# Keeping half a granule more between two layers: folded w2, packed tiny tiles, rows in a lent annex, and V as the weight around a turn

## The chip, the cores and the metric

The kernel runs on one core of one Trainium2 chip; the chip's other cores do nothing for it. The metric is the device time of one execution in microseconds (us), less is better. TensorE is the matmul engine, VectorE and ScalarE the two elementwise engines, GpSimd the small general one; the DMA engines, sixteen for the core, bring data from HBM, the chip's main memory, into SBUF, the core's own memory. PSUM is the small memory that TensorE writes its results to.

## The reference, cut to what matters

The model is two layers over the same caches: attention of one query token over 4096 cached keys and values, 32 heads, 8 batch rows, then a small feed-forward block. The second round reads the same caches and weights as the first.

```python
B, Sq, D = 8, 1, 640
Hq, Hkv, Sk, Dh = 32, 32, 4096, 128
...
x = x + _A_ref(_layernorm(x), k_cache, v_cache, wq, wo)   # layer 0
x = x + _B_ref(_layernorm(x), w1, w2)                     # Dff = 1728
x = x + _A_ref(_layernorm(x), k_cache, v_cache, wq, wo)   # layer 1, same caches
x = x + _B_ref(_layernorm(x), w1, w2)
```

The caches hold 537 MB in bf16, so reading them once per layer is 1074 MB. What is still in SBUF when layer 1 of a batch row begins need not be read again.

## The kernel before

The caches pass through an arena of 26 slots in SBUF. A slot holds a granule: a quarter of the keys (or of the values) of a pair of heads, 4 KB on each of 128 partitions, 512 KB in all. A visit is one pair of heads of one batch row in one layer: it takes four granules of K, makes a softmax, then takes four of V. A Python function plans everything ahead: the order of visits, which slot each load goes into, and how many granules one load takes.

The **turn** of a batch row is where its layer 1 begins. The pairs visited last in layer 0 are visited first in layer 1, in reversed order. At a turn 21 granules stay in the arena and 3 more are stashed in PSUM banks and a 2 KB annex, so for a while only five slots are free and loads are single granules. In this document t is the first visit of a turn, and t+4 the fifth. The kernel has eight turns; seven of them lie between two batch rows, and per-turn means are over these seven.

```python
order1 = list(range(NP - 1, NP - 4, -1)) + list(range(NP - 3))
...
moving = [not any(t - AHEAD - 1 <= i < t + 5 for t in turns) and i < NV - 2 for i in range(NV)]
direct = [i == NV - 1 or visits[i][0] == 0 and last_of[visits[i][:2]] == i for i in range(NV)]
...
keep = set(first[: G - SPARE])                       # 21 granules
stash = first[G - SPARE : G - SPARE + STASH]         # 3 more
```

A visit's K product is *wide* where `moving` is true (the cache streams as the moving operand, 4 matmuls of 512 columns a granule) and *narrow* near a turn (the cache is the weight, 16 matmuls of one column a granule). V is wide too, unless the visit is *direct*: then V is the weight. Each matmul comes with a weight load, so a wide granule costs 8 TensorE instructions and a narrow or direct one 32.

```python
if which == "V":
    for c in range(4):
        h, j = c // 2, g * VJ + c % 2 * CJ
        for n in range(CJ) if direct[i] else ():
            nc.tensor.matmul(o2_ps[h], lhsT=arena[...128x128 of V...], rhs=P_tiles[i][:, h, j + n : j + n + 1], ...)
        if direct[i]:
            continue
        nc.tensor.matmul(o_ps[32 * c : 32 * c + CJ, :], lhsT=P_tiles[i][:, h, j : j + CJ],
                         rhs=arena[...512 columns of V...], ...)
```

A wide V is evicted by ScalarE into a row tile (`o_sb`) and gathered by four matmuls; a wide K leaves its exponentials in a row tile too (`P_row`). Both rows share one buffer of 1 KB.

Of the kernel before, what the change touches and what calls it, by code (L numbers as in the profile page):

```python
# [16 lines left out]
UNIT = 4  # L17
GP = 4
# [17 lines left out]
def plan(B, NP, n_up, n_down):  # L36
# [5 lines left out]

    order0 = list(range(NP))
    order1 = list(range(NP - 1, NP - 4, -1)) + list(range(NP - 3))
# [12 lines left out]
    moving = [not any(t - AHEAD - 1 <= i < t + 5 for t in turns) and i < NV - 2 for i in range(NV)]  # L57
    last_of = {(layer, b): v for v, (layer, b, hp) in enumerate(visits)}
    direct = [i == NV - 1 or visits[i][0] == 0 and last_of[visits[i][:2]] == i for i in range(NV)]
# [7 lines left out]
    stash = first[G - SPARE : G - SPARE + STASH]  # L67
# [8 lines left out]
    for which, i in slots:  # L76
        layer, b, hp = visits[i]
        uses += [(which, i, g) for g in range(UNIT)]
        stream += [(which, i, g) for g in range(UNIT) if layer == 0 or (which, hp, g) not in keep | set(stash)]
# [26 lines left out]

    def place(x):

        return visits[x[1]][1], tile_at(NP, x[0], visits[x[1]][2]) * UNIT + x[2]
# [6 lines left out]
    def feed():  # L116

        while at[0] < len(stream):
            lead = clock[1] - clock[0]
            calm = (PACE * (nth[stream[at[0]]] - at[1]) - LATE - lead) / 1.2  # L120
            least = next((n for us, n in LEADS if lead >= us), 1)
            least = min(least, max(1, (G - len(kept) - 2) // 3))
            most = min(max(least, int(calm)), LEADS[0][1], max(1, (len(stream) - at[0]) // 2))
            least = min(least, most)
            b, p = place(stream[at[0]])
            n = 1
            while n < most and place(stream[at[0] + n]) == (b, p + n):
                n += 1
            least = min(n, least)
            u = next((u for n in range(n, least - 1, -1) if (u := room(n)) is not None), None)  # L130
            if u is None:
                return
            n = next(k for k in range(n, 0, -1) if room(k) == u)
            for k, (which, i, g) in enumerate(stream[at[0] : at[0] + n]):
                ops.extend(("weights",) + w for w in weights.pop(i, []) if which == "K")
                owner[u + k] = True
                where[which, i, g] = u + k
                if keeps(which, i, g):
                    kept[which, b, visits[i][2], g] = u + k
            at[0] += n  # L140
            clock[1] = max(clock[1], clock[0] + 1.4) + 0.1 + 1.2 * n
            lands[u : u + n] = [clock[1] + 2] * n
            ops.append(("load", b, p, n, u))
# [5 lines left out]
    def release(which, i, g):  # L149
        key = which, visits[i][1], visits[i][2], g  # L150
        u = where.pop((which, i, g), None)
        at[1] += 1
        if key in kept:
            if visits[i][0] == 0:
                return
            u = kept.pop(key)
        if visits[i][0] == 0 and stashed(which, i, g) is not None:
            ops.append(("stash", stashed(which, i, g), u))
        owner[u], freed[u] = False, at[1]
        x = uses[at[1] + SOON] if at[1] + SOON < len(uses) else None  # L160
        if x and visits[x[1]][0] and stashed(*x) is not None:
            u = where[x] = room(1)
            owner[u] = True
            lands[u] = clock[0] + 2
            ops.append(("unstash", stashed(*x), u))
        feed()
# [130 lines left out]
def kernel(  # L297
# [31 lines left out]
    f_sizes = [min(P, Dff - f * P) for f in range(FC)]  # L329
# [11 lines left out]
    annex = sm.tile([P, 2 * BANK], BF16, name="annex", bufs=1)  # L341
    lent = [2 * BANK]

    def temp(shape, dtype, name):

        if shape[1] == 1:
            return sm.tile(shape, dtype, name=name, bufs=1)
        n = int(np.prod(shape[1:])) * (2 if dtype == FP32 else 1)
        lent[0] -= -(-n // 16) * 16
        assert lent[0] >= 0  # L350
        t = annex[: shape[0], lent[0] : lent[0] + n]
        t = t.bitcast(FP32) if dtype == FP32 else t
        return t.rearrange("p (a b) -> p a b", a=shape[1]) if len(shape) == 3 else t
# [6 lines left out]
    w2_sb = wres.tile([P, FC, D], BF16, name="w2_sb")  # L360
# [5 lines left out]
    def load_weights(which, g=0):  # L366
        if which == "wq":
            nc.sync.dma_start(out=wq_sb[:, g], in_=wq_src[:, g])
        elif which == "wo":
            h0, h1 = g * 2 * GP, (g + 1) * 2 * GP  # L370
            nc.sync.dma_start(out=wo_sb[:, h0:h1, :], in_=wo_src[:, h0:h1, :])
        elif which == "w1":
            nc.sync.dma_start(out=w1_sb, in_=B_w1.rearrange("p (c f) -> p c f", c=DC))
        else:
            nc.sync.dma_start(out=w2_sb, in_=B_w2.rearrange("p (f n) -> p f n", f=FC))
# [41 lines left out]
    o2_ps = o_ps[:, :1], s_ps[:, 8 * NJ - 1 : 8 * NJ]  # L417
    per = GW // (2 * BANK)
    stash_ps = ps.tile([P, (STASH * per - 1) * 2 * BANK], BF16, name="stash_ps")
    stash = [stash_ps[:, n * 2 * BANK : (n + 1) * 2 * BANK] for n in range(STASH * per - 1)] + [annex]  # L420
    assert len(stash) > DC
# [35 lines left out]
    def inverse_root(out, s2, k):  # L457

        v = sm.tile([P, 4], FP32, name="root", bufs=1)
# [15 lines left out]
    def do_ws(closing):  # L475

        for n, hp in enumerate(closing):
            ws = sm.tile([P, 2], FP32, name="wsum", bufs=1)
# [52 lines left out]
    def finish_steps(layer, b):  # L531
# [13 lines left out]
        def up(k):  # L545
            for f in up_parts[k]:
                fs = f_sizes[f]
                for c in range(DC):
                    nc.tensor.matmul(
                        h[k][:fs, f, :], lhsT=w1_sb[:, c, f * P : f * P + fs], rhs=st["xf"][:, :, c],  # L550
                        start=(c == 0), stop=(c == DC - 1),
                    )
# [7 lines left out]
        def root():  # L560
            if layer:
                st["rstd"] = root_of_all(var_ps[:, :nb])
            else:
                st["rstd"] = sm.tile([P, 1], FP32, name="rstd", bufs=1)
                inverse_root(st["rstd"], var_ps[:, :1], 1.0)

        def relu(k=None):
# [3 lines left out]
            for rows, lo, hi in ((P, part[0], min(part[-1] + 1, n_full)), (Dff % P, n_full, part[-1] + 1)):  # L571
                if rows and lo < hi:
                    nc.vector.tensor_scalar(
                        out=st["hT"][:rows, lo:hi], in0=h[k or 0][:rows, lo:hi], scalar1=0.0, scalar2=None, op0=ALU.max
                    )

        def down(k):
            for c, f in [(k, f) for f in range(FC)] if layer == 0 else [(c, f) for f in up_parts[k] for c in range(DC)]:
                fs = f_sizes[f]
                nc.tensor.matmul(  # L580
                    y[:, c, :], lhsT=w2_sb[:fs, f, c * P : (c + 1) * P], rhs=st["hT"][:fs, f, :],
                    start=(f == 0), stop=(f == FC - 1),
                )

        def add():
            yT = y.rearrange("p c b -> p b c")
            if layer == 0:
                nc.vector.scalar_tensor_tensor(out=x, in0=yT, scalar=st["rstd"], in1=x, op0=ALU.mult, op1=ALU.add)
                s1 = sm.tile([P, 1], FP32, name="s1", bufs=1)
# [10 lines left out]
        def center():  # L600
            xc = sm.tile([P, 1, DC], FP32, name="xc", bufs=1)
# [3 lines left out]
            xlns[b] = sm.tile([P, 1, DC], BF16, name="xq", bufs=2)  # L605
# [3 lines left out]
        def root2():  # L609
            r = q_scale[b] = sm.tile([P, 2], FP32, name="q_scale", bufs=2)  # L610
# [12 lines left out]
    def do_stash(slot, u):  # L623
        for n, t in enumerate(stash[slot * per : (slot + 1) * per]):
# [6 lines left out]
    def do_unstash(slot, u):  # L631
        for n, t in enumerate(stash[slot * per : (slot + 1) * per]):
# [3 lines left out]
    def do_load(b, p, n, u):  # L636
        nc.sync.dma_start(out=arena[:, u * GW : (u + n) * GW], in_=A_kv[b, :, p * GW : (p + n) * GW])

# [10 lines left out]

    def do_q(b, hp):  # L650
        q_ps = st["q", b, hp] = q2_ps if hp == NP - 1 else q1_ps[:, 2 * (hp % 2) : 2 * (hp % 2) + 2]
# [21 lines left out]
    def do_mm(which, i, g, u):  # L673
        layer, b, hp = visits[i]
        at = u * GW
        if which == "V":
            for c in range(4):
                h, j = c // 2, g * VJ + c % 2 * CJ
                for n in range(CJ) if direct[i] else ():
                    nc.tensor.matmul(  # L680
                        o2_ps[h], lhsT=arena[:, at + (c * CJ + n) * Dh : at + (c * CJ + n + 1) * Dh],
                        rhs=P_tiles[i][:, h, j + n : j + n + 1],
                        start=(j + n == 0), stop=(j + n == NJ - 1),
# [26 lines left out]
    def do_m1(i):  # L710
        m_tiles[i] = sm.tile([P, 2], BF16, name="mrow")
# [12 lines left out]
    def do_m2(i):  # L724
        if moving[i]:
            nmax[i] = sm.tile([2, 2], BF16, name="diag")
# [4 lines left out]
        hmx = sm.tile([2, 1], FP32, name="hmx")  # L731
        nc.vector.tensor_reduce(out=hmx, in_=turn_ps, axis=AX.X, op=ALU.max)  # L732
        nmax[i] = sm.tile([2, 2], BF16, name="diag")
# [13 lines left out]
    def do_e(i):  # L747
        nm = sm.tile([P, 2], FP32, name="nmax")
        layer, b, hp = visits[i]
        less, more = (q_scale[b][:, 1:2], q_scale[b][:, 0:1]) if layer else (-inv_sqrt_dh, inv_sqrt_dh)  # L750
        if moving[i]:
            less, more = (less[:OR], more[:OR]) if layer else (less, more)
            nc.scalar.activation(out=nm[:OR, :1], in_=max_ps[:OR, :1], func=ACT.Copy, scale=less)  # L753
            P_rows[i] = sm.tile([P, BANK], BF16, name="P_row", tag="row", bufs=1)
# [30 lines left out]
    def do_i(i):  # L785
        L = sm.tile([P, 2], FP32, name="lsum")
# [3 lines left out]
        invL[i] = sm.tile([P, 2], FP32, name="invL", bufs=3)  # L790
        nc.vector.reciprocal(out=invL[i], in_=L)

    def do_oc(i):
        o_tiles[i] = sm.tile([P, CJ, Dh], BF16, name="o_sb", tag="row", bufs=1)
# [9 lines left out]
    def do_o(i):  # L804
# [3 lines left out]
        else:  # L808
            dst = oT[i] = sm.tile([P, 2], BF16, name="oT")
# [5 lines left out]
        for h, o in enumerate(o2_ps):  # L815
            nc.vector.tensor_tensor(out=dst[:, h : h + 1], in0=o, in1=L[:, h : h + 1], op=ALU.mult)

# [31 lines left out]
    does = dict(WS=do_ws, S=do_s, SM=do_sm, SC=do_sc, YC=do_yc, load=do_load, stash=do_stash, unstash=do_unstash, weights=load_weights, mm=do_mm, M1=do_m1, T=do_t, M2=do_m2, B=do_b, E=do_e,  # L849
                L=do_l, I=do_i, OC=do_oc, OG=do_og, O=do_o, W=do_w, Y=do_y, C=do_finish, Q0=do_q0, Q=do_q, QC=take_q, QZ=do_qz, PT=do_pt, PC=do_pc, clear=do_clear)  # L850

    with tc.manual_schedule(engines={ENG.PE, ENG.DVE, ENG.Activation, ENG.Pool, ENG.SP}):
# [4 lines left out]
        lent[0] = 2 * BANK  # L857
# [9 lines left out]
def _laid_out(A_x, A_k_cache, A_v_cache, A_wq, A_wo, B_w1, B_w2):  # L867
# [5 lines left out]
    NP, NJ, DC, NG, FC = H // 2, Sk // p, D // p, H // 2 // GP, -(-Dff // p)  # L873
    c = np.ascontiguousarray
    w2 = np.zeros((FC * p, D), B_w2.dtype)
    w2[:Dff] = B_w2
# [3 lines left out]
    for hp in range(NP):  # L880
# [9 lines left out]
        "B_w2": c(w2.reshape(FC, p, D).transpose(1, 0, 2)).reshape(p, -1),  # L890
# [26 lines left out]
```

## Time and profile before

Median 2341.5 us over 6 runs (2338.0 to 2343.1).

| what | value | view |
|---|---|---|
| span of the profiled run | 2343.0 us | page |
| bytes read from HBM | 988.08 MB | page, DMA queues |
| TensorE busy | 60% | page |
| steady stretch | 432 GB/s | windows |
| just before a turn | 395 GB/s in the turn shown | windows |

The page of the kernel before. The first lines give span and busy time; the next three cut the span into 40 slices (granted TensorE clock and DMA busy share in tenths, and GB/s); then the DMA queues (packets, MB, share of 16 engines) and the chain of work that ended last.

```profile
span 2343.0 us, 43024 instructions
PE 1398.6 (60%) x18748; PEld 591.4 (25%) x18748; DVE 496.7 (21%) x2022; ACT 426.3 (18%) x986; POOL 59.5 (3%) x296
...
PEclk9999999999999998555555555555555555555555
DMA  9999999999999999999999999999999999999997
GB/s 411 430 433 401 433 432 432 431 396 432 432 432 430 404 434 431 430 427 403 433 432 431 426 412 434 430 432 420 427 431 427 432 416 430 431 431 431 396 433 329
...
q1 hardware_dynamic: 76564, 988.12, 99.4%
q8 instruction: 146, 2.39, 0.4%
q14 instruction: 43, 0.35, 0.0%
...
DMA 71%; PE 17%; ACT 6%; DVE 3%; issue 2%; SPq 0%; POOL 0%; ACTq 0%; DVEq 0%; POOLq 0%
```

The DMA engines are busy in every slice, and the slices between turns, the first and last aside, stay at 426 to 435 GB/s on both sides of the halved clock; the regular dips are the turns. The profiled run itself took 2344.8 us, longer than any of the six timed runs.

The groups of instructions of the kernel before: line, engine, operation, tiles and shapes, count, then busy us and mean ns of one, then idle before them. L687 is wide V, L680 direct V (one of its two halves), L795 the eviction of V.

```profile
L687 PE MATMUL o_ps<-arena,P_sb 128*4 128x512 bf16 x3952 | 584.3, 596 | 402.0 <-DMA arena<-in_A_kv_dram 401.0
L795 ACT CAST o_sb<-o_ps 100x512 bf16<-100x512 f32 x247 | 144.9, 587 | 289.3 <-PE o_ps L687 286.0 <-PE small_ps L781 2.5
L680 PE MATMUL o_ps<-P_sb,arena 128*128 128x1 bf16 x288 | 12.9, 166 | 7.5 <-DMA arena<-in_A_kv_dram 4.3 <-ACT o_sb L795 3.0
```

### The profile page before, as it was taken

The numbers are of one execution on the slowest core, as the hardware profiler recorded it, in microseconds if no ns is written. First come the engines' busy times: TensorE is split into PE (matmuls) and PEld (weight loads), VectorE is DVE, ScalarE is ACT, GpSimd is POOL, SyncE is SP. The second block draws the span as 40 slices with busy tenths as digits, with TensorE's granted clock in tenths as the row PEclk, the third lists the DMA queues.
The fourth block names the chain that finished last, engine by engine and source line by source line (L and its number), as shares of the span: only waits on it lengthen the run. The fifth ranks groups of instructions, "written<-read, shape, count | busy, mean of one in ns | idle before, by whom it ended". The sixth has DMA issues, their size and how long they took to land.

```text
span 2343.0 us, 43024 instructions
## 1 busy us (share of the span) xinstructions
PE 1398.6 (60%) x18748; PEld 591.4 (25%) x18748; DVE 496.7 (21%) x2022; ACT 426.3 (18%) x986; POOL 59.5 (3%) x296
## 2 busy tenths in 40 slices
PE   3547654576545764557545675556755567545766
PEld 1214211152111511125111241113411133111523
DVE  1113211131112211122111221112211122111312
ACT  1111211122111221112211121111211112111211
POOL 0000000000000000000000000000000000000000
PEclk9999999999999998555555555555555555555555
DMA  9999999999999999999999999999999999999997
GB/s 411 430 433 401 433 432 432 431 396 432 432 432 430 404 434 431 430 427 403 433 432 431 426 412 434 430 432 420 427 431 427 432 416 430 431 431 431 396 433 329
DMA packets 76753, 990.87 MB, mean 423 GB/s; under 512 B 8596, under 2 KB 8596, under 8 KB 36500
## 3 DMA queue, kind: packets, MB, share of 16 engines
q1 hardware_dynamic: 76564, 988.12, 99.4%
q8 instruction: 146, 2.39, 0.4%
q14 instruction: 43, 0.35, 0.0%
HBM read 988.08 MB, written 0.01 MB: 422 GB/s over the span
## 4 chain that ended last, share of the span: by engine, by line
DMA 71%; PE 17%; ACT 6%; DVE 3%; issue 2%; SPq 0%; POOL 0%; ACTq 0%; DVEq 0%; POOLq 0%
DMA arena<-in_A_kv_dram 71%; PE o_ps L687 5%; PE s_ps L695 4%; PE s_ps L705 2%; ACT P_row L755 2%; ACT o_sb L795 1%; PE small_ps L655 1%; DVE mrow L713 1%; ACT P_sb L761 1%; PE small_ps L800 1%; ACT arena L634 1%; PE small_ps L768 1%; PE small_ps L825 1%; DVE hmx L732 0%; ACT nmax L753 0%
## 5 line engine op out<-in xcount | busy, mean ns | idle before, releaser
L687 PE MATMUL o_ps<-arena,P_sb 128*4 128x512 bf16 x3952 | 584.3, 596 | 402.0 <-DMA arena<-in_A_kv_dram 401.0
L695 PE MATMUL s_ps<-arena,qz 128*4 128x512 bf16 x3040 | 410.3, 602 | 261.1 <-DMA arena<-in_A_kv_dram 249.5
L687 PEld LDWEIGHTS <-P_sb 128*4 128x4 bf16 x3952 | 107.4, 88 | 502.8 <-issue 491.7
L713 DVE TENSOR_REDUCE mrow<-s_ps 100x1 bf16<-100x512 f32 x190 | 131.8, 694 | 323.2 <-PE s_ps L695 323.2
L795 ACT CAST o_sb<-o_ps 100x512 bf16<-100x512 f32 x247 | 144.9, 587 | 289.3 <-PE o_ps L687 286.0
L753 ACT ACTIVATE nmax<-small_ps 100x1 f32<-100x1 f32 x106 | 18.1, 171 | 774.5 <-PE small_ps L742 774.5
L775 DVE CAST P_sb<-small_ps 128x64 bf16<-128x64 f32 x190 | 42.6, 224 | 523.1 <-PE small_ps L768 523.1
L695 PEld LDWEIGHTS <-qz 128*4 128x4 bf16 x3040 | 63.9, 85 | 313.7 <-issue 295.5
L705 PEld LDWEIGHTS <-arena 128*128 128x128 bf16 x4224 | 129.6, 104 | 40.8 <-DMA arena<-in_A_kv_dram 23.4
L705 PE MATMUL s_ps<-qo,arena 128*128 128x1 bf16 x3712 | 123.7, 165 | 17.2 <-ACT P_sb L761 7.6
L768 PE MATMUL small_ps<-few,P_row 100*128 100x16 bf16 x760 | 52.3, 179 | 92.1 <-ACT P_row L755 92.1
L753 ACT ACTIVATE nmax<-small_ps,q_scale 100x1 f32<-100x1 f32 x84 | 22.0, 261 | 398.7 <-PE small_ps L742 398.7
L787 DVE TENSOR_REDUCE lsum<-small_ps 128x2 f32<-128x64 f32 x240 | 53.9, 224 | 171.9 <-PE small_ps L781 171.9
L768 PEld LDWEIGHTS <-P_row 100*128 100x128 bf16 x760 | 35.0, 107 | 186.5 <-ACT P_row L755 178.2
L720 PE MATMUL small_ps<-few,mrow 100*1 100x16 bf16 x190 | 34.4, 181 | 67.6 <-DVE mrow L713 67.6
L755 ACT ACTIVATE P_row<-s_ps,nmax 100x512 bf16<-100x512 f32 x106 | 72.8, 687 | 3.4
L800 PEld LDWEIGHTS <-o_sb 100*128 100x128 bf16 x988 | 45.7, 106 | 107.2 <-ACT o_sb L795 73.8
L655 PE MATMUL small_ps<-xq,wq_sb 128*128 128x1 bf16 x1200 | 48.8, 165 | 38.9 <-DVE qo L812 33.5
L800 PE MATMUL small_ps<-few,o_sb 100*128 100x2 bf16 x988 | 65.1, 170 | 10.7 <-DVE lsum L787 2.2
L727 DVE TENSOR_REDUCE diag<-small_ps 1x2 bf16<-1x16 f32 x190 | 30.8, 162 | 186.9 <-PE small_ps L720 186.9
L720 PEld LDWEIGHTS <-mrow 100*1 100x1 bf16 x190 | 15.0, 79 | 210.8 <-DVE mrow L713 210.8
L755 ACT ACTIVATE P_row<-s_ps,nmax,q_scale 100x512 bf16<-100x512 f32 x84 | 65.3, 778 | 2.8
(225 smaller groups left out, 958.0 us busy)
## 6 DMA issues: line engine op xcount, KB each, us to landing
arena<-in_A_kv_dram SPq DMA_DIRECT2D x124, 4096.0 KB, 23.1
arena<-in_A_kv_dram SPq DMA_DIRECT2D x98, 2048.0 KB, 22.7
arena<-in_A_kv_dram SPq DMA_DIRECT2D x218, 512.0 KB, 6.5
arena<-in_A_kv_dram SPq DMA_DIRECT2D x48, 1024.0 KB, 11.3
arena<-in_A_kv_dram SPq DMA_DIRECT2D x11, 3072.0 KB, 22.4
arena<-in_A_kv_dram SPq DMA_DIRECT2D x11, 2560.0 KB, 20.5
arena<-in_A_kv_dram SPq DMA_DIRECT2D x10, 1536.0 KB, 19.7
wq_sb<-in_A_wq_dram SPq DMA_DIRECT2D x4, 1280.0 KB, 17.6
```

Source lines behind the costliest of these rows:

```text
L655: nc.tensor.matmul(q_ps[:, h : h + 1], lhsT=wq_sb[:, g, c, (2 * n + h) * Dh : (2 * n + h + 1) * Dh], rhs=xlns[b][:, 0, c : c + 1], start=( ...
L687: nc.tensor.matmul(o_ps[32 * c : 32 * c + CJ, :], lhsT=P_tiles[i][:, h, j : j + CJ], rhs=arena[:, at + c * CJ * Dh : at + (c + 1) * CJ * D ...
L695: nc.tensor.matmul(s_ps[32 * c : 32 * c + CJ, :], lhsT=qz[:, i % 3, c // 2, 3 - g : 3 - g + CJ], rhs=arena[:, at + c * BANK : at + (c + 1) ...
L705: nc.tensor.matmul(s_tiles[i][:, j : j + 1], lhsT=arena[:, at + n * P : at + (n + 1) * P], rhs=qo[:, b, h : h + 1], start=True, stop=True,)
L713: nc.vector.tensor_reduce(out=m_tiles[i][:OR, :1], in_=s_ps[:OR], axis=AX.X, op=ALU.max)
L720: nc.tensor.matmul(turn_ps[:1, : 4 * CJ], lhsT=m[:OR, :1], rhs=rsel[:OR], start=True, stop=True)
L755: nc.scalar.activation(out=P_rows[i][:OR], in_=s_ps[:OR], func=ACT.Exp, bias=nm[:OR, :1], scale=more)
L768: nc.tensor.matmul(P_ps[:, k * 4 * CJ : (k + 1) * 4 * CJ], lhsT=P_row[:OR, k * P : (k + 1) * P], rhs=rsel[:OR], start=True, stop=True,)
L775: nc.vector.tensor_copy(out=P_tiles[i].rearrange("p h (c k) -> p h c k", k=BANK // P), in_=P_ps.rearrange("p (k h c) -> p h c k", k=BANK / ...
L787: nc.vector.tensor_reduce(out=L, in_=(lsum2_ps if ahead[i] else lsum_ps).rearrange("p (h j) -> p h j", h=2), axis=AX.X, op=ALU.add)
L795: nc.scalar.copy(out=o_tiles[i][:OR], in_=o_ps[:OR, :].rearrange("p (j d) -> p j d", j=CJ))
L800: nc.tensor.matmul(oy[i][:, :2], lhsT=o_tiles[i][:OR, j, :], rhs=gsel[:OR, j, :], start=(j == 0), stop=(j == CJ - 1))
```

## The change

The intent is to read less: half a granule more of each batch row is kept between its layers. The room for it comes from several places.

- w2's last rows (64 of 128 partitions used) are folded, which saves 512 B a partition, and many tiny tiles are packed into one.
- The annex grows from 2 to 4 KB. Its lower half holds the two rows, `P_row` and `o_sb`, each with 1 KB of its own; at a turn this half is lent to kept V. While it is lent, no visit may use a row. So the window of narrow visits moves one visit earlier (t-4 to t+3 instead of t-3 to t+4), and V is the weight from t-5 to t+1: 57 direct visits instead of 9.
- Layer 1 starts with four pairs in reversed order instead of three. Of the fourth pair's V, half of the last granule is kept in a PSUM bank; the other half is loaded (`rest`).

The diff is cut to these places:

```diff
-    order1 = list(range(NP - 1, NP - 4, -1)) + list(range(NP - 3))
+    order1 = list(range(NP - 1, NP - 5, -1)) + list(range(NP - 4))
-    moving = [not any(t - AHEAD - 1 <= i < t + 5 for t in turns) and i < NV - 2 for i in range(NV)]
+    moving = [not any(t - AHEAD - 2 <= i < t + 4 for t in turns) and i < NV - 2 for i in range(NV)]
-    direct = [i == NV - 1 or visits[i][0] == 0 and last_of[visits[i][:2]] == i for i in range(NV)]
+    direct = [i == NV - 1 or any(t - AHEAD - 3 <= i < t + 2 for t in turns) for i in range(NV)]
-    stash = first[G - SPARE : G - SPARE + STASH]
+    stash = first[G - SPARE : G - SPARE + STASH] + [("V", order1[3], UNIT - 1)]
...
-    annex = sm.tile([P, 2 * BANK], BF16, name="annex", bufs=1)
+    annex = kv.tile([P, 4 * BANK], BF16, name="annex")
+    row_P, row_o = annex[:, :BANK], annex[:, BANK : 2 * BANK]
...
+    tiny = kv.tile([P, 64], FP32, name="tiny")            # and few_of(), which cuts tiny tiles from it
-    w2_sb = wres.tile([P, FC, D], BF16, name="w2_sb")
+    w2_sb = wres.tile([P, n_full * D + fold * P], BF16, name="w2_sb")
...
-    o2_ps = o_ps[:, :1], s_ps[:, 8 * NJ - 1 : 8 * NJ]
+    o2_ps = o_ps[:, :2]
+    halves_of = banks[1:] + [annex[:, : 2 * BANK], annex[:, 2 * BANK :]]
+    stash = [halves_of[n * per : (n + 1) * per] for n in range(STASH)] + [banks[:1]]
...
+    def do_rest(b, p, u):
+        nc.sync.dma_start(
+            out=arena[:, u * GW + 2 * BANK : (u + 1) * GW], in_=A_kv[b, :, p * GW + 2 * BANK : (p + 1) * GW]
+        )
...
+            if direct[i] and g == 0:
+                nc.tensor.matmul(o2_ps, lhsT=ident, rhs=qz[:, 0, 0, :2], start=True, stop=False)
```

## The prediction

> **What bounds the kernel now.** The DMA engines. The page's slices show them 90% busy or more in every slice but the last (70%), while TensorE is 60% busy, VectorE 21%, ScalarE 18%. The chain that ended last is 71% DMA into the arena. In steady stretches the windows show 430 to 433 GB/s; the Trainium skill, "DMA: Bandwidth & Descriptors", Specifications, gives 435 GB/s as the fabric ceiling, and the trace agrees: its packets took 159 ns for 4096 B, 611 ns for 16384 B and 1213 ns for 32768 B, a straight line of 36.8 ps per byte (16 engines: 435 GB/s) plus 8.4 ns a packet. The halved granted clock from about 930 us on doesn't change those rates, so TensorE isn't the limit. Only three things are not pure streaming: some 2.5 us before the first transfer, 13 us after the last one, and the eight turns, where rates drop to 352 to 415 GB/s over about 40 us each. There 21 of the 26 granules are kept, and loads are single granules (4096 B a row, at best 409 GB/s by the packets) that each wait for a granule to be released. Packets in flight add up to about 5.5 us of engines standing empty over all turns.
>
> **What the change does.**
> 1. Eight batches each load half a granule (256 KB) less: 1856 to 1852 granules by the plan. By the packet line a single load costs an engine 8x159+9 = 1.28 us, a half one 8x84+9 = 0.68 us: 0.60 us a turn, 4.8 us in all. With the slightly different cutting (521 to 520 loads) the plan's sums are 2275.3 and 2270.5 us: -4.9 us. This is on the critical path whole, if the queue doesn't run dry.
> 2. w2 rows shrink from 17920 to 17408 B: -0.15 us.
> 3. V is the weight in 57 visits instead of 9. A granule costs TensorE the same: 16 narrow matmuls took 0.58 us, 4 wide ones 0.60 us. But 48 evictions (0.587 us on ScalarE) with their four gathering matmuls leave, so o_ps comes free sooner at the turns, where loads wait on releases. Estimate: 0 to 1.5 us less.
> 4. Added: 8 half stashes (0.69 us each on VectorE) and 8 half unstashes (1.01 us each on ScalarE), both engines mostly idle; off the path, unless the copy waits for its arena slot with softmax work behind it.
> 5. P_row and o_sb no longer share one buffer: shortens compute chains, which hide under streaming.
> 6. Tail: five more narrow matmuls (about 0.15 us), one relu piece and one scaling less: within 0.3 us of nothing.
>
> **Prediction.** About -5.2 us: 2336.5 us, -0.2%. Range 2330 to 2342, widened for the spread of before (2338 to 2343). Chances: faster by over 2% 0.01, within 2% 0.98, slower by over 2% 0.01.
>
> **What would show it.** HBM read falls by about 2.16 MB from 988.1 MB to 985.9 MB. Steady stretches keep 430 to 433 GB/s. The distance from turn to turn falls by 0.6 us (about 286.6 us before). Rates within turns stay or rise slightly, and the wait of the DMA queue for o_ps matmuls shrinks there. The time after the last transfer stays 13 us. Evictions fall from 247 to 199; o_ps direct matmuls rise from 576 to 3648. If rates at the turns rise well above before, term 3 was too small; if they fall, term 4 is wrong.
>
> **What would make it wrong.** The unstash or the half load waiting for its slot and draining the queue (1 us a turn would undo it all); added in-order waits through the annex, which now holds rows and stash; packing tiny tiles making false dependencies; or a shorter recirculation delay at the turns giving more than 5.5 us of empty engines and slowed packets back, for some -10 us.

## More of the kernel before

The windows view of the kernel before at one turn, whose first K product starts at 1365 us: 25 to 5 us before it, 15 to 35 us after it, and 60 to 160 us after it. The last columns are granted clock, DMA share and GB/s.

```profile
1340.00:1360.00 20.00, 16.34 (x391) 12.89 (x388) 5.55 (x33) 2.00 (x8) 2.33 (x11) 0.50 1.01 395
1380.00:1400.00 20.00, 15.17 (x256) 7.32 (x248) 5.62 (x21) 8.76 (x20) 0.00 (x0) 0.50 1.01 431
1425.00:1525.00 100.00, 54.31 (x520) 16.19 (x521) 17.25 (x65) 18.18 (x38) 1.16 (x6) 0.50 1.00 432
```

The queues q8 and q14, of the kind `instruction`, carry programs and not data.

## The result, and the profile after

Median 2345.7 us over 6 runs (2343.9 to 2346.5) against 2341.5 us: ratio 1.0019, with a 95% interval of 1.0006 to 1.0032. Ratios here are the mean time of one kernel's fast runs over the mean of the other's fast runs of the same rounds, so not quite the ratio of the medians. The kernel is 0.2% slower; the prediction was 0.2% faster, and the time lies outside its range.

The page of the changed kernel, the same lines:

```profile
span 2344.2 us, 47218 instructions
PE 1380.4 (59%) x20962; PEld 655.4 (28%) x20962; DVE 496.4 (21%) x2012; ACT 405.0 (17%) x946; POOL 57.9 (2%) x288
...
q1 hardware_dynamic: 76420, 985.96, 99.3%
q8 instruction: 163, 2.67, 0.4%
q14 instruction: 41, 0.34, 0.0%
...
DMA 71%; PE 19%; ACT 4%; DVE 3%; issue 2%; SPq 0%; DVEq 0%; ACTq 0%; POOL 0%; POOLq 0%
```

The 2.16 MB are gone as planned (988.12 to 985.96 MB on q1), TensorE's busy time even fell, and yet the span is longer. There are 4194 more instructions, and q8 carries 163 packets instead of 146.

The groups of the changed kernel: L729 is wide V, L837 its eviction, L722 direct V.

```profile
L729 PE MATMUL o_ps<-arena,P_sb 128*4 128x512 bf16 x3184 | 477.9, 596 | 178.5 <-DMA arena<-in_A_kv_dram 178.5
L837 ACT CAST annex<-o_ps 100x512 bf16<-100x512 f32 x199 | 116.6, 586 | 213.5 <-PE o_ps L729 213.2
L722 PE MATMUL o_ps<-P_sb,arena 128*128 128x1 bf16 x3648 | 128.0, 166 | 37.1 <-DMA arena<-in_A_kv_dram 30.4 <-issue 5.1
```

768 wide matmuls became 3072 direct ones, and 48 evictions went, exactly as forecast.

The windows view of the changed kernel at the same turn, which starts at 1362 us here, with the same three distances:

```profile
1337.00:1357.00 20.00, 16.01 (x453) 14.45 (x454) 5.06 (x29) 1.45 (x7) 2.34 (x11) 0.50 1.00 392
1377.00:1397.00 20.00, 14.63 (x219) 6.38 (x218) 6.13 (x21) 7.29 (x16) 0.00 (x0) 0.50 0.99 395
1422.00:1522.00 100.00, 52.70 (x519) 16.77 (x519) 16.75 (x64) 17.59 (x37) 1.16 (x6) 0.50 1.00 431
```

The steady stretch is as fast as before. After the turn there is a gap: 395 GB/s where the kernel before had 431 (over seven turns, 414.7 against 430.0).

The prediction expected the DMA queue's wait for matmuls into `o_ps` to shrink at the turns. The waits of the DMA queue (SPq) around the same turn, 25 us before it to 35 us after it, show who was waited for, us in total, how often, and the longest us; first the kernel before, then the changed kernel:

```profile
SPq L637 <- PE o_ps L687: 4.2, 5, 1.6
SPq L637 <- PE o_ps L705: 2.5, 4, 0.6
```

```profile
SPq L668 <- PE o_ps L722: 6.0, 6, 2.0
SPq L668 <- PE o_ps L747: 2.4, 4, 0.6
SPq L668 <- PE o_ps L729: 0.6, 1, 0.6
```

These sums are 6.7 and 9.0 us. Over the seven turns their means are 13.8 us before and 15.8 after, with single turns between 7 and 23 us: the wait did not shrink.

The last load lands 10.6 us before the end of the span in both kernels, so the tail is innocent: the DMA stream itself lost what the saved bytes gave.

From the packets of the trace one can see that no packet line changed: 159 ns for 4096 B and 1213 ns for 32768 B in both kernels. The summed best-case times of all data packets, over 16 engines, fell from 2310.7 to 2305.7 us, the 5.0 us that were forecast. What grew are stretches in which fewer than 16 packets are in flight, and packets that take longer than their size asks for.

### The profile page after: what moved, and what is told of

It is laid out like the page before. It is cut to its first block, busy times and chain, and to the rows that moved or that the text cites. A ratio compares the mean times of both kernels' runs of the same rounds, so it can differ in the third digit from the quotient of the medians.

```text
span 2344.2 us, 47218 instructions
## 1 busy us (share of the span) xinstructions
PE 1380.4 (59%) x20962; PEld 655.4 (28%) x20962; DVE 496.4 (21%) x2012; ACT 405.0 (17%) x946; POOL 57.9 (2%) x288
## 3 DMA queue, kind: packets, MB, share of 16 engines
q1 hardware_dynamic: 76420, 985.96, 99.3%
HBM read 985.92 MB, written 0.01 MB: 421 GB/s over the span
## 4 chain that ended last, share of the span: by engine, by line
DMA 71%; PE 19%; ACT 4%; DVE 3%; issue 2%; SPq 0%; DVEq 0%; ACTq 0%; POOL 0%; POOLq 0%
DMA arena<-in_A_kv_dram 71%; PE s_ps L737 7%; PE o_ps L729 3%; PE s_ps L747 2%; ACT annex L797 2%; DVE tiny L755 2%; PE o_ps L722 1%; PE small_ps L695 1%; PE small_ps L842 1%; PE small_ps L810 1%; ACT P_sb L803 1%; PE small_ps L866 1%; ACT tiny L795 1%; PE small_ps L784 0%; PE small_ps L762 0%
## 5 line engine op out<-in xcount | busy, mean ns | idle before, releaser
L729 PE MATMUL o_ps<-arena,P_sb 128*4 128x512 bf16 x3184 | 477.9, 596 | 178.5 <-DMA arena<-in_A_kv_dram 178.5
L755 DVE TENSOR_REDUCE tiny<-s_ps 100x1 bf16<-100x512 f32 x190 | 131.8, 694 | 262.5 <-PE s_ps L737 262.5
L729 PEld LDWEIGHTS <-P_sb 128*4 128x4 bf16 x3184 | 84.9, 91 | 257.9 <-issue 250.1
L837 ACT CAST annex<-o_ps 100x512 bf16<-100x512 f32 x199 | 116.6, 586 | 213.5 <-PE o_ps L729 213.2
L722 PE MATMUL o_ps<-P_sb,arena 128*128 128x1 bf16 x3648 | 128.0, 166 | 37.1 <-DMA arena<-in_A_kv_dram 30.4
L747 PEld LDWEIGHTS <-arena 128*128 128x128 bf16 x4224 | 130.8, 104 | 67.4 <-DMA arena<-in_A_kv_dram 46.7
L797 ACT ACTIVATE annex<-s_ps,tiny 100x512 bf16<-100x512 f32 x190 | 138.9, 731 | 6.2
L722 PEld LDWEIGHTS <-arena 128*128 128x128 bf16 x3648 | 113.4, 105 | 57.9 <-DMA arena<-in_A_kv_dram 41.8
L810 PE MATMUL small_ps<-few,annex 100*128 100x16 bf16 x760 | 52.3, 179 | 101.9 <-ACT annex L797 101.9
L810 PEld LDWEIGHTS <-annex 100*128 100x128 bf16 x760 | 35.0, 107 | 197.2 <-ACT annex L797 195.1
L829 DVE TENSOR_REDUCE tiny<-small_ps 128x2 f32<-128x64 f32 x240 | 53.6, 223 | 122.4 <-PE small_ps L823 122.4
L866 PEld LDWEIGHTS <-wo_sb 128*128 128x128 bf16 x1440 | 51.7, 105 | 59.5 <-issue 59.5
```

The costliest lines, as they stand in the source:

```text
L722: nc.tensor.matmul(o2_ps[:, h : h + 1], lhsT=arena[:, at + (c * CJ + n) * Dh : at + (c * CJ + n + 1) * Dh], rhs=P_tiles[i][:, h, j + n : j ...
L747: nc.tensor.matmul(s_tiles[i][:, j : j + 1], lhsT=arena[:, at + n * P : at + (n + 1) * P], rhs=qo[:, b, h : h + 1], start=True, stop=True,)
L755: nc.vector.tensor_reduce(out=m_tiles[i][:OR, :1], in_=s_ps[:OR], axis=AX.X, op=ALU.max)
L797: nc.scalar.activation(out=P_rows[i][:OR], in_=s_ps[:OR], func=ACT.Exp, bias=nm[:OR, :1], scale=more)
L810: nc.tensor.matmul(P_ps[:, k * 4 * CJ : (k + 1) * 4 * CJ], lhsT=P_row[:OR, k * P : (k + 1) * P], rhs=rsel[:OR], start=True, stop=True,)
L829: nc.vector.tensor_reduce(out=L, in_=(lsum2_ps if ahead[i] else lsum_ps).rearrange("p (h j) -> p h j", h=2), axis=AX.X, op=ALU.add)
```

## The experiments

Three theories were on the table first. **W**: the shifted window makes the compute after the turn slower, so slots come free late. **H**: the half granule's own copies and its early slot. **L**: the planner cuts loads worse. **D** and **O** followed: V as weight, or the new order. All experiments ran 5 rounds (5 or 6 runs of each kernel) with 9 or 11 runs of the kernel before on the same chip. One run scatters by some 2 us, so a ratio's interval is about 0.0013 wide to each side; effects below 3 us are judged by the trace, too. The edits below are shortened.

### One narrow visit more in the changed kernel

```diff
-    moving = [not any(t - AHEAD - 2 <= i < t + 4 for t in turns) ...
+    moving = [not any(t - AHEAD - 2 <= i < t + 5 for t in turns) ...
```

> The changed kernel with visit t+4 (the fifth visit from the turn on, t being the first visit of layer 1) narrow again as before the change, so one more narrow visit. Theory W (the shifted window slows the compute after the turn, so arena slots come free late and the DMA queue empties at about 16 to 30 us after the turn): the gap there shrinks, time falls from 2345.7 to 2337 to 2341 us. Rival H (the half granule's own copies and its early slot cause the gap): gap stays, 2344 to 2347 us. Rival L (load cutting by the plan, 4-granule loads waiting for the last of four slots, causes it): between, as the cutting changes too (3 and 3 granules instead of 2 and 4).

Measured: 2346.6 us, ratio to before 1.0022 (1.0009 to 1.0034). The compute is faster again (the fifth visit's K starts 22.9 us after the turn's, on average; 23.6 in the changed kernel, 22.7 before), but nothing is gained. W falls as the main cause.

### The changed kernel without the half granule

```diff
-    stash = first[...] + [("V", order1[3], UNIT - 1)]
+    stash = first[...]
```

> The changed kernel without the half granule: the last granule of that V is loaded whole, all else, including the order and cutting of the loads, is the same (1 where the half was). Theory W: only bytes come back, plus 4.8 us: 2350 us. Rival H: the 4.8 us of bytes are offset by the loss of the harm, 2342 to 2346 us, and the gaps after the turn go. Theory L: 2350 us as W, since the cutting is the same.

Measured: 2348.7 us, ratio 1.0030 (1.0017 to 1.0042). Loading the half costs about 2.6 us by the ratios (0.0011 of 2341 us), and 4.6 us between the two profiled runs' last landings. The intervals of the two ratios overlap, but both measures say that keeping the half granule helps and neither that it harms, so H falls; something else in the change costs 7 us.

### The kernel before with the shifted window alone

```diff
-    moving = [not any(t - AHEAD - 1 <= i < t + 5 for t in turns) ...
+    moving = [not any(t - AHEAD - 2 <= i < t + 4 for t in turns) ...
```

> The kernel before with nothing changed but the window of narrow visits, shifted one visit earlier (t-4 to t+3 instead of t-3 to t+4), with practically the same loads. Theory W: slower by 3 to 7 us than before, with gaps after the turn as in the changed kernel. H and L: within 1 us of before.

Measured: 2343.0 us, ratio 1.0005 (0.9992 to 1.0018). The compute after the turn slowed as much as in the changed kernel (23.7 us to the fifth visit), yet the stream kept 429.7 GB/s 15 to 35 us after the turns, on average. A slower pace alone is absorbed.

### A more honest planning clock in the changed kernel

```diff
-    clock[1] = max(...) + 0.1 + 1.2 * n
+    clock[1] = max(...) + 0.1 + (0.6 if <the half load> else 1.2 * n)
```

> The changed kernel, whose planning clock now counts the half load as half a granule (0.6 us) instead of a whole one. That changes only how loads are cut and when they are issued. Theory L: the planned lead is more honest, loads after the turn are cut smaller, time falls by 2 to 5 us to 2341 to 2344 us. W: the same within 1.5 us, 2344 to 2347 us. H: the same.

Measured: 2345.3 us, ratio 1.0016 (1.0004 to 1.0028). The cutting changed (504 loads instead of 512, besides the eight half loads), the time did not. L gets no support.

### V as the weight alone, the order alone, and neither

The first takes the direct visits of the changed kernel into the kernel before; the second its order; the third is the changed kernel without half, direct visits and shifted window, but with folded w2, packed tiles and separate rows.

```diff
 # g1: the kernel before, plus
+    direct = [i == NV - 1 or any(t - AHEAD - 3 <= i < t + 2 for t in turns) for i in range(NV)]
 # g2: the kernel before, plus
+    order1 = list(range(NP - 1, NP - 5, -1)) + list(range(NP - 4))
 # f1: the changed kernel, with direct and moving as before, no half, rows never lent
```

> The kernel before with one part of the change alone: V is the weight in the 57 visits of the changed kernel instead of 9 (with the one accumulation that it starts for both heads). Theory D (using V as weight is what costs: more instructions to fetch, about 1 us of DMA time, and slower compute around the turns): 3 to 7 us over before, 2344 to 2348 us, instruction fetch up by 0.28 MB. Theory O (the order of layer 1, four pairs turned round instead of three, and the load cutting that follows from it): only the fetch, 2341 to 2342.5 us.

> The kernel before with the order of layer 1 alone changed (pair 12 fourth after the turn), which also changes how loads are cut there to nearly the cutting of the changed kernel. Theory O: 3 to 7 us over before, 2344 to 2348 us, with new gaps in the DMA stream 16 to 30 us after the turn. Theory D: within 1 us of before.

> The changed kernel less the half granule, the direct visits and the shifted window: it keeps the folded w2, the packed tiny tiles, rows with a buffer each in an annex that is not lent there, and the new order; its loads are the same as those of the order-alone kernel. Theory D: as before, 2340.5 to 2342.5 us. Theory O: 2344 to 2348 us, like order alone. Rival P (packing or rows in the annex cost through false waits): this one slow, and both single-part kernels about as before.

Measured: V as weight alone 2345.6 us, ratio 1.0019 (1.0005 to 1.0032); order alone 2342.0 us, ratio 1.0000 (0.9988 to 1.0013); neither 2342.1 us, ratio 1.0008 (0.9995 to 1.0020). D holds: making V the weight costs about 4.5 us all by itself, as much as the whole change lost. O and P (false waits) have no support. One thing beside V changed in the first run: the planner cut its loads differently (512 instead of 521). No run tests that alone; the idle-instruction run below has the old cutting and loses as much.

The profile of V as weight alone: its span and busy line, the instruction queue, and the windows 25 to 5 us before and 60 to 160 us after the same turn.

```profile
span 2346.5 us, 47280 instructions
PE 1388.4 (59%) x20917; PEld 658.7 (28%) x20917; DVE 495.3 (21%) x2013; ACT 397.8 (17%) x938; POOL 59.0 (3%) x296
...
q8 instruction: 163, 2.67, 0.4%
```

```profile
1341.00:1361.00 20.00, 15.24 (x431) 13.62 (x429) 5.04 (x30) 1.27 (x6) 2.31 (x11) 1.00 1.00 383
...
1426.00:1526.00 100.00, 53.85 (x519) 16.92 (x519) 17.10 (x64) 18.16 (x38) 1.15 (x6) 1.00 1.01 433
```

TensorE is busy 10 us less than before and the steady stretch runs at 433 GB/s, but just before the turn the stream is at 383 GB/s where it was at 395 (over seven turns, 374.4 against 388.9). This run even had the full granted clock throughout, so the clock is not it. What grew is the number of TensorE instructions: 4338 rows of its program more, and 17 more packets on q8. The Trainium skill, "Perfetto Trace Analysis", section "The 4-stage abstract model", says that instructions are 64 bytes; 4338 x 64 B is 17 packets of the 16 KB that q8's packets have in the trace. So the numbers agree with q8 being where TensorE's program is fetched.

### Idle TensorE instructions in place of V as weight

If the fetch is the cost, instructions that do nothing must cost the same, far away from any turn too.

```diff
 # i1: at each K granule of visits t+9 to t+21, six times; i2: at V granules of t-5 to t+1, twelve times
+    nc.tensor.matmul(small_ps[:, 508:509], lhsT=ident, rhs=qz[:, 0, 0, :1], start=True, stop=True)
```

> The kernel before plus about as many TensorE instructions as the direct visits add (4368 rows more, against 4338), but as idle 128x1 matmuls into an unused column, put into the 13 visits in the middle of each steady stretch, far from the turns. Theory I (the extra instructions must be fetched by DMA; a fetch packet holds up one of the 16 engines, a load ends with its slowest engine, so the stream loses more than the mean of 1 us): 2 to 5 us over before, 17 more packets of the instruction queue. Theory C (direct visits slow the compute or the release of slots around the turns): within 1 us of before.

> The kernel before plus idle matmuls in those visits in which the changed kernel has V as weight (48 a visit, 4032 rows more), V itself as before. Theory I: 3 to 6 us over before, as V-as-weight alone was (1.0019). Theory C: no prediction apart from I if the added TensorE time (about 1.4 us a visit) also delays; if this is over 8 us, the time of TensorE at the turns counts too.

Measured, far from the turns: 2344.9 us, ratio 1.0018 (1.0005 to 1.0030). Theory I's forecast holds and C's fails: 4368 idle instructions in the middle of the steady stretches cost as much as the direct visits. At the turns: 2395.5 us, ratio 1.0230 (1.0216 to 1.0244), far over the 8 us mark. 2016 idle pairs there cost 54.7 us, 27 ns each, which is the pace at which pairs of a weight load and a narrow matmul run back to back (48 in 1.28 us in the chain of the kernel before). So at a turn added TensorE time lies on the critical path, which the prediction's "TensorE isn't the limit" left out. That it counts whole is not shown: the 54.7 us also hold the fetch of 16 more packets on q8, and waits may be among them, since the idle pairs write a PSUM tile that other engines read, and 38.4 us of TensorE's idle time stand before them in the trace.

The profile of the first of these, span, busy line and q8, then the windows before the same turn and in the stretch that holds idle instructions:

```profile
span 2346.1 us, 47425 instructions
PE 1509.2 (64%) x20932; PEld 673.1 (29%) x20932; DVE 496.7 (21%) x2022; ACT 425.7 (18%) x986; POOL 59.0 (3%) x296
...
q8 instruction: 163, 2.67, 0.4%
```

```profile
1342.00:1362.00 20.00, 15.91 (x391) 12.84 (x388) 5.63 (x33) 1.89 (x8) 2.31 (x11) 0.50 0.98 383
...
1427.00:1527.00 100.00, 65.70 (x759) 25.43 (x756) 17.07 (x64) 18.14 (x38) 1.15 (x6) 0.50 1.00 431
```

The stretch with the idle work streams at 431 GB/s, but 25 to 5 us before the turn, more than 70 us after the last idle matmul, the stream is at 383, with a DMA share of 0.98. The cost is incurred in one place and paid in another. The idle pairs had waits here too (59.2 us of TensorE's idle time stand before them), so slower compute is not excluded by this run alone; that the stretch itself streams at full rate speaks against it.

### Fewer TensorE instructions in the changed kernel

```diff
 # i4, wrong result on purpose: layer 0's output projection, all visits but a row's last
-    ten matmuls of lhsT=wo_sb[:, 2 * hp + h, c * P : (c + 1) * P]
+    one matmul of lhsT=wo_sb[:, 2 * hp, :P] into all five columns
```

> The changed kernel with 2160 TensorE instructions fewer: the output projection of layer 0, off the critical path in the steady stretches, does one matmul in place of ten in each visit but the last of a row; the result is wrong on purpose. Theory I: 1.5 to 3 us less than the changed kernel, ratio to before 1.0006 to 1.0012, 8 packets of the instruction queue fewer. Theory C: the same as the changed kernel, 1.0019, within 0.0004.

Measured: 2340.3 us, ratio 0.9998 (0.9985 to 1.0010), with 155 packets on q8. The direction is I's, the size is larger than expected (5 us, against 1.5 to 3). This run takes TensorE time away from the turns as well, where the run above shows that it counts, so it does not measure the fetch alone.

### A quarter granule without lending anything

```diff
 # q1: the changed kernel, direct and moving as before
+    row_P = row_o = annex[:, :BANK]
+    stash = [...] + [[annex[:, BANK : 2 * BANK]]]        # a quarter granule; the rest load takes three quarters
```

> A version meant to beat both: the folded w2 and packed tiny tiles stay, but the rows get 1 KB of their own, shared as before, so nothing is lent, V is the weight in 9 visits only, and a quarter of a granule is kept instead of half. Bytes say -2.4 us and -0.15 us against before at the same number of TensorE instructions: theory I 2337.5 to 2340 us, ratio 0.9985 to 0.9995.

Measured: 2340.5 us, ratio 0.9997 (0.9984 to 1.0009). It gains less than hoped and is not shown to beat the kernel before; it is ahead of the changed kernel (1.0019 in its own rounds; the two intervals just overlap).

### Double dose, another engine, and time without instructions

What remained open was whether the number of TensorE instructions costs, or fetching in general, or TensorE's time.

```diff
 # j1: as i1, twelve times instead of six
 # j2: the kernel before, at each K granule of all wide visits, six times
+    nc.gpsimd.memset(scratch, 0.0)
 # j3: the kernel before, in the visits of i1, at two of four K granules
+    nc.tensor.matmul(stash_ps.bitcast(FP32)[:, :BANK], lhsT=ident, rhs=arena[:, at : at + BANK], ...)
```

> The kernel before plus twice as many idle TensorE instructions in the middle of the steady stretches as in the earlier run (8736 rows more instead of 4368, which cost 1.0018). Theory I (fetch traffic): the cost doubles, ratio 1.003 to 1.0045, 34 packets of the instruction queue more than before. Rival E (idle matmuls slow the compute of those visits, or a step, not the number of instructions): no doubling, or far more than a doubling.

> The kernel before plus 24 one-element memsets on GpSimd in each of the 190 wide visits (4560 instructions), TensorE untouched. Theory I: fetches are fetches, whichever engine reads them: some 17 packets more and 2 to 5 us over before, ratio 1.001 to 1.002. Rival E (it is the TensorE work, not the fetch): within 0.0005 of before.

> The kernel before plus two idle 512-column matmuls in each of the same 91 visits in the middle of the steady stretches: at least as much TensorE time there as the 24 narrow pairs added, but only 364 rows instead of 4368. Theory IT (what costs is fetching TensorE instructions: the fetch packets leave single DMA engines behind, and the lag is paid at the next turn): one or two packets more, within 0.0005 of before. Rival E (TensorE work there delays the stream): 1.001 to 1.003.

Measured: the double dose 2347.9 us, ratio 1.0028 (1.0016 to 1.0041); the GpSimd memsets 2341.4 us, ratio 1.0002 (0.9989 to 1.0014); the wide idle matmuls 2340.3 us, ratio 0.9999 (0.9986 to 1.0013). The double dose again costs clear of noise; whether twice the single dose can't be said, since 1.0036 and 1.0018 both lie in its interval. The cost does not come with TensorE's time: the wide idle matmuls add 76 us of busy time in 364 rows, at no cost that shows (they write another PSUM tile than the narrow pairs, so waits for that tile are not tested apart). And "fetches are fetches", as theory I had it, finds no support: GpSimd's instructions cost nothing measurable, though the interval, up to 1.0014, overlaps that of TensorE's, from 1.0005.

The double dose, the GpSimd memsets and the wide idle matmuls, span, busy line and instruction queues:

```profile
span 2347.1 us, 51793 instructions
...
q8 instruction: 180, 2.95, 0.4%
```

```profile
span 2340.2 us, 47502 instructions
PE 1397.3 (60%) x18748; PEld 590.9 (25%) x18748; DVE 496.3 (21%) x2022; ACT 426.2 (18%) x986; POOL 520.0 (22%) x4856
...
q8 instruction: 146, 2.39, 0.4%
q14 instruction: 78, 0.64, 0.1%
```

```profile
span 2338.4 us, 43388 instructions
PE 1474.9 (63%) x18930; PEld 597.0 (26%) x18930; DVE 496.0 (21%) x2022; ACT 426.2 (18%) x986; POOL 59.5 (3%) x296
...
q8 instruction: 148, 2.42, 0.4%
```

TensorE's instructions come on q8 in packets of 16 KB that took 933 ns on average; GpSimd's came on q14 in packets of 8 KB that took 320 ns. A data packet of 16 KB took 611 ns.

**Where the lag sits.** The Trainium skill, "DMA: Bandwidth & Descriptors", section "Why a DMA increments its semaphore by 16 and not by 1", says that each engine that takes part in a load counts up the semaphore once its share has landed, and that a load is complete only at 16. The trace records all sixteen landings of each load, so one can see how far the slowest engine is behind: call lag the last landing minus the mean of the sixteen. The table has the largest lag 20 to 10 us before a turn, and 0 to 15 us after its start, both as a mean over seven turns (loads whose sixteen landings could not be paired in the trace, 134 of 533 in the kernel before, are left out), with the mean GB/s of the window 25 to 5 us before the turn (seven answers of the windows view).

| kernel | q8 packets | lag before turn, us | after, us | GB/s before turn | ratio |
|---|---|---|---|---|---|
| before | 146 | 1.96 | 1.66 | 388.9 | 1 |
| order alone | 146 | 2.09 | 1.55 | 385.3 | 1.0000 |
| GpSimd memsets | 146 | 1.89 | 1.47 | 392.3 | 1.0002 |
| wide idle matmuls | 148 | 1.89 | 1.49 | 387.9 | 0.9999 |
| V as weight alone | 163 | 2.59 | 1.68 | 374.4 | 1.0019 |
| idle pairs, far from turns | 163 | 2.46 | 1.60 | 377.0 | 1.0018 |
| idle pairs, double | 180 | 2.51 | 1.42 | 375.1 | 1.0028 |
| changed kernel | 163 | 2.15 | 1.33 | 386.9 | 1.0019 |

With more TensorE instructions some engine comes to a turn 2.5 us behind instead of 1.9, and after the turn all kernels are at about 1.5, which fits a lag that is settled there. The rates before the turns have the size of the loss: (388.9 - 377.0) / 388.9 x 20 us is 0.6 us a turn with idle pairs, and 0.75 us with V as weight, 4 to 5 us over seven turns. Evenly spread over 16 engines, 17 packets of 0.933 us would cost 1.0 us; they cost 4. The reading that fits best: a fetch packet holds up one engine; in the steady stretch deep queues let each engine go on by itself, so that nothing is lost; at the turn only a few single granules are in flight, each complete only with its slowest engine, and the other engines stand idle until it has caught up. The same skill page, section "Queues, rings and completion order", says that each engine takes its queue rows in turn, packet by packet; the 933 against 611 ns agree with a fetch sharing its engine with data. Which engines the fetches go to, the trace does not record, so this last step is argued and not shown. It also leaves something unexplained: with the double dose, neither the lag (2.51 against 2.46 us) nor the rate before the turns (375.1 against 377.0) moved further.

### What else the changed kernel lost

In the changed kernel's own profile the loss sits elsewhere: before the turns it has 386.9 GB/s, nearly as before, but 15 to 35 us after them 414.7 against 430.0. V as weight alone has 429.0 there, order alone 427.3.

```diff
 # h1: the kernel before, plus new order and shifted window; q2: the quarter-granule kernel with t + 4 for t + 5 in moving
```

> The kernel before with the new order of layer 1 and the shifted window of narrow visits together, V as before (neither alone cost anything: 1.0000 and 1.0005). Theory G (together they open the small gap in the DMA stream 15 to 25 us after a turn that the changed kernel shows, 0.4 to 0.6 us a turn): gap there in the trace, 1.0008 to 1.0020. Otherwise: 0.9995 to 1.0006 and no gap.

> The quarter-granule version with one narrow visit fewer after each turn (t-3 to t+3), which takes away 688 TensorE rows (three packets or so). Theory I: 0.5 us less than the quarter-granule version, ratio to before 0.9985 to 0.9997; if the slower wide visit after the turn costs more, 1.000 or above.

Measured: order and window together 2342.4 us, ratio 1.0009 (0.9996 to 1.0022), with 422.9 GB/s in that window; the quarter-granule kernel with one narrow visit fewer 2343.2 us, ratio 1.0006 (0.9993 to 1.0020), with 420.6 GB/s there (427.9 with all its narrow visits). The gap shows in the traces; the times alone do not clear it. The kernel with a narrow visit more (the first experiment) still had 415.9 GB/s, so the missing narrow visit t+4 is not needed for it when V is the weight. No kernel without the new order shows the gap (V as weight together with the shifted window, in the old order, was not tried), and with the new order it is larger where the window is shifted or V is the weight; more than that is not settled.

The changed kernel's one profile shows little of the loss before the turns, but three experiments that are nearly the same kernel do show it, next to the gap: with one narrow visit more, without the half granule and with the other planning clock (163 to 166 packets on q8), the stream has 381.9, 377.1 and 379.9 GB/s before the turns, and 415.9, 419.9 and 422.6 after them. So both losses occur together in this design; their split varies from profile to profile.

## Why the prediction was wrong

1. **What bounds the kernel: half right.** "TensorE isn't the limit" holds in the steady stretches, where 76 us of idle TensorE work cost nothing. It fails at the turns: 2016 idle pairs there cost 54.7 us, about what their own time is.
2. **Bytes: right.** HBM read fell by 2.16 MB to 985.92 MB, the best-case packet sum by 5.0 us (4.9 and 0.15 were forecast). Taking the half out again cost 2.6 us by the ratios (not clear of noise), 4.6 us by the profiled runs' last landings.
3. **The step that failed is the third: "V is the weight in 57 visits instead of 9. A granule costs TensorE the same", with "Estimate: 0 to 1.5 us less".** The durations were right and TensorE's busy time fell by 18 us in the changed kernel. But the gain it named did not come: with 48 evictions gone, the DMA queue's wait for `o_ps` matmuls at the turns did not shrink (13.8 us a turn before, 15.8 after). And it costed time and not instructions: the 48 visits add 4338 rows of TensorE program, and V as weight alone costs 4.5 us (1.0019) where 0 to 1.5 us of gain were expected. Idle instructions in their number, far away, cost the same (1.0018). That their number costs is shown in three kernels (1.0018 to 1.0028, with controls at 0.9999 to 1.0002); how, by the lag of single DMA engines, is argued.
4. **Stashes and unstashes: right.** The copies took 0.69 and 1.01 us as forecast. Without them and the half the kernel was slower, not faster. The prediction's own test, "if they fall, term 4 is wrong", named the wrong suspect: rates after the turns did fall, by the gap described last.
5. **Separate rows: no gain seen**, as said (1.0008 with them and neither half nor direct visits, not clear of 1).
6. **Tail: right.** 10.6 us from the last landing to the end in both kernels (the prediction had put it at 13 us).
7. **The distance from turn to turn** was to fall by 0.6 us. Its mean from the first to the seventh turn is 286.2 us before and 286.1 us after: the lag and the gap took it back.

The sum as far as it goes: -5.0 us of bytes, +4.5 us for TensorE's instructions, and some 2 to 5 us for the gap after the turns (order and window: 0.0009 of 2341 us; in the changed kernel (430.0 - 414.7) / 430 x 20 us is 0.7 us a turn). That gives +1.5 to +4.5 us against the measured 0.0019, 4.4 us. The parts were measured in different kernels, each within about 3 us, and the split between the last two inside the changed kernel stays open: in its one profile the lag before turns is 2.15 us, less than where V as weight was added alone, and its near copies divide the loss otherwise.

## What to carry to other kernels

In a kernel that streams at the DMA limit, count TensorE's instructions too: swapping 4 wide matmuls for 16 narrow ones cost no engine time here and still cost the stream 4.5 us; the likely reason is that the instructions are fetched by DMA as well. Look at the profile's instruction queues next to the data queues, and at the places where few loads are in flight, for that is where the loss showed here. To test such a suspicion, put idle instructions where they can do no other harm, and then the same time without the instructions.

## What the Trainium skill lacked or had wrong

- "Runtime: NRT & Kernel Launch", "Instruction fetch mechanics", describes the fetch, in 16 KiB blocks over a DMA queue of the sequencer's own, and calls the cost of crossing a block "mostly hidden". It gives no time for a block and does not say what fetching costs a data stream at the DMA limit. Here TensorE's fetch ran on queue 8 with 146 packets of 16 KB, 933 ns each (a data packet of that size: 611 ns), and 17 more of them, around the turns or far from them, cost about 4 us of 2341.
- "DMA: Bandwidth & Descriptors" explains why a load waits for its slowest engine but not how far behind that engine can be in a stream of loads. Here it was 1.9 us behind the mean before turns, 2.5 us with more TensorE instructions, and about 1.5 us after turns (means of the largest lag at seven turns).
- No page gives the fetch cost of one engine beside another's: 4560 more GpSimd instructions came on queue 14 in 35 packets of 8 KB, 320 ns each, with a ratio of 1.0002 (0.9989 to 1.0014); for TensorE's it was 1.0018 (1.0005 to 1.0030).
- "DMA: Bandwidth & Descriptors", Specifications, gives 435 GB/s as the ceiling of the fabric; this case agrees, with 431 to 433 GB/s in steady stretches and 435 GB/s by the slope of its packet times.
